# Neighbouring score blocks, earlier normed and turned tiles, and three more fillers in a chunk-attention and Fourier-mix kernel

## The chip, the cores and the metric

The kernel runs on one core of a Trainium2 chip. The metric is the device time of one execution in microseconds. Three runs of the kernel before gave 1109.81 (median), 1108.6 and 1110.18 us. The profiled execution took 1109.99 us, of which 1108.2 us lie between its first and last instruction.

## What is computed

Attention within chunks of 64 tokens, then a mixing block with two Fourier transforms, a normalisation and a two-layer perceptron. All data are float32, with q, k, v of 8 batches x 8 heads x 576 tokens x 64.

```python
scores = scale * matmul(q_c, k_c.T)             # per chunk of 64 tokens
attn   = softmax(scores)
x      = matmul(attn, v_c)                      # then to (B, S, 512)
mixed  = real(fft(fft(x, axis=1), axis=2))
u      = x + mixed
un     = (u - mean(u)) / sqrt(var(u) + 1e-6)
out    = u + relu(un @ w_ch1) @ w_ch2           # 512 -> 2048 -> 512
```

## The kernel before

**Tiles and groups.** Tokens are handled in 36 tiles of 128 (two chunks). A batch has four tiles of its own ("lo" and "hi", two each, since the Fourier transform folds a token with its mirror image), and every two batches share a "rest" tile. Even batches therefore have five tiles in this order and odd ones four. The perceptron works on groups of four tiles: one group for each batch, and a ninth for the four rest tiles.

**Two streams in one program.** The order of every engine's instructions is written out by hand. The loop at L1189 runs the perceptron of group g step by step (`mlp`), and after each step it advances a generator, `side(b)`, that does the attention of batch b (`attention`), three empty steps, and its Fourier part (`fourier`). So the batch g+1 is prepared while group g is in the perceptron. Each engine works its list off in order; semaphores between the engines are set by the framework.

**The perceptron's forms.** Group 0 uses plain products. From group 1 on the down product (`down_halves`, L1042) and from group 2 on the up product (`up_halves`, L997) use seven products of half size instead of eight, numbered o = 0 to 6. Each is done for r = 0 and 1, and k = 2o + r counts these in the down half. A step of the down half is eight float32 matmuls on TensorE, which are 16 passes. The results are summed from PSUM by VectorE and ScalarE, on lines L1018 to L1035 and L1065 to L1082. The operands for the down half are made ahead by `operands` (L916 to L920). Converted weights are written to DRAM by `keep1` and `keep2` during groups 0 and 1, through buffers that share the places `wb` and `yall` with those operands, and fetched again by `fetch`.

**Attention of a tile** (from batch 2 on). `att_T` transposes q and k on VectorE (L348) and loads the next tile's q and k. `att_S` (L380) makes the scores, 32 small passes in a 64x64 mode. `softmax` (L393, L395) takes maximum and difference on VectorE, `exponential` is on ScalarE. `att_P` transposes the weights on TensorE (L329). `att_V` (L428) weights the values, 32 small passes again, into two PSUM buffers of the pool `ps_t`, and VectorE divides (L441 to L445). In the loop of `attention`, the scores of tile n+1 stand right behind the weighting of tile n, except for a batch's first tile, whose scores open the batch's generator.

**From one group to the next.** While group g is in its down half, the tiles of group g+1 are finished: `fourier` adds the mixed part and takes means (L712, L632, L633, with the reciprocal deviation at L637), `normed` (L824) makes `un`, `turned` (L329, then L835 or L837) transposes it through a `ps_t` buffer into `unT`, and `combined` (L845 to L848) makes three sums of it for the seven products. `normed` of tile j is asked for after step k = 4 + 2j, `turned` after step k = 5 + 2j.

**The start.** Batch 0 is done by `attention_early` and `fourier_early`. Where TensorE has nothing to do there, `keep_warm` puts in fillers: matmuls on zeros whose result is not used (L1142).

Of the kernel before, what the change touches and what calls it, by code (L numbers as in the profile page):

```python
# [16 lines left out]
def kernel(  # L17
# [39 lines left out]
    NT = 2 * 2 * NM + 1  # L57
# [315 lines left out]
    def att_S(n):  # L373
        a, b = qT.pop(n), kT.pop(n)
        sc = ps_a.tile([128, 2, 512], FP32, tag="att", name="sc")
        for j in range(NJ):
            for e in range(2):
                for c in range(2):
                    r0, t0 = e * D, c * CH
                    nc.tensor.matmul(  # L380
                        out=sc[t0:t0 + CH, e, j * CH:(j + 1) * CH],
                        lhsT=a[r0:r0 + D, 2 * j + c, 0:CH],
                        rhs=b[r0:r0 + D, 2 * j + c, 0:CH],
                        start=True,
                        stop=True,
                    )
        scs[n] = sc
# [139 lines left out]
    def attention_early():  # L527

        lo, hi = first[0], first[1] - 1

        def ready(n):
            if n == at[LO, 0, 1]:
                shift_early(0)
            if n == at[HI, 0, 1]:
                fold(0, 1)
            if n == at[HI, 0, 0]:
                fold(0, 0)
            if n + 3 > hi:
                load_v(n + 3)

        att_T(lo)
        att_S(lo)
        for n in range(lo, hi + 1):
            if n < hi:
                att_T(n + 1)
            softmax(n)
            if n > lo:
                att_V(n - 1)
                ready(n - 1)
            if n < hi:  # L550
                att_S(n + 1)
            if n in (lo, hi):
                keep_warm(1)
            att_P(n)
        shift_early(1)
        fold(0, NM)
        keep_warm(1)
        att_V(hi)
        ready(hi)
        keep_warm(3)  # L560
        turn_tables()
        round_next()
        round_next(put_off)

    def attention(b):

        lo, hi = first[b], first[b + 1] - 1

        def ready(n):

            if n == at[LO, b, NM - 1]:
                shift(b)
            for i in range(NM):
                if n == at[HI, b, i]:
                    fold(b, i)
            if n == at[HI, b, 0]:
                fold(b, NM)
            return kind(n) == HI

        if b > 1:  # L580


            att_S(lo)
            softmax(lo)
            yield
            for n in range(lo, hi + 1):
                exponential(n)
                if n + 1 < NT:
                    att_T(n + 1, "q")
                yield  # L590
                att_P(n)
                if n + 1 < NT:
                    att_T(n + 1, "k")
                yield
                att_V(n)
                if n < hi:
                    att_S(n + 1)
                    softmax(n + 1)
                if n + 3 < NT:
                    load_v(n + 3)  # L600
                yield ready(n)
            return
        att_T(lo)
        yield
        for n in range(lo, hi + 1):
            att_S(n)
            softmax(n)
            yield
            if n + 1 < NT:
                att_T(n + 1)  # L610
            yield
            if n > lo:
                att_V(n - 1)
                if n + 2 < NT:
                    load_v(n + 2)
                yield ready(n - 1)
            att_P(n)
            yield
        att_V(hi)
        if hi + 3 < NT:  # L620
            load_v(hi + 3)
        yield ready(hi)
# [204 lines left out]
    def turned(g, s):  # L827
        if s >= len(groups[g]):
            return
        if s == 0:  # L830
            unTs[g] = one_p.tile([128, KD, G * 128], FP32, tag="unT", name="unT")
        unT, un = unTs[g], uns.pop((g, s))
        pt = turn(lambda j: un[:, j * 128:(j + 1) * 128])
        if s % 2 and g > 1:
            nc.vector.tensor_copy(unT[:, :, s * 128:(s + 1) * 128], pt)  # L835
        else:
            nc.scalar.copy(unT[:, :, s * 128:(s + 1) * 128], pt)  # L837
# [204 lines left out]
    def down_halves(g, h1):  # L1042
        pas, pbs = {}, {}
        for o in range(NO):
            w = slab2[((g - first_of[2]) * NO + o) % NS2]
            for r in range(2):
                cl, ch = slice(r * 128, (r + 1) * 128), slice(256 + r * 128, 256 + (r + 1) * 128)
                low, high = groups[g][r], groups[g][2 + r]
                olow, ohigh = os_[:, 2 * r], os_[:, 2 * r + 1]
                a, b = tmp[:, r, 0], tmp[:, r, 1]  # L1050
                if o == 0:
                    pas[r] = ps_f.tile([128, 2, 256], FP32, tag="ff", name="pa")
                if o == 2:
                    pbs[r] = ps_f.tile([128, 2, 256], FP32, tag="ff", name="pb")
                dst = (pas, pas, pbs, pbs, pas, pbs, pbs)[o][r][:, (0, 1, 0, 1, 0, 0, 1)[o]]
                lhs = (
                    h1[:, 0:HF, cl], ys[:, :, cl], xs[:, :, cl], h1[:, 0:HF, ch],
                    h1[:, HF:KF, cl], ys[:, :, cl], h1[:, HF:KF, ch],
                )[o]
                for m in range(HF):  # L1060
                    nc.tensor.matmul(  # L1061
                        out=dst, lhsT=lhs[:, m], rhs=w[:, m],
                        start=(o in (0, 2) and m == 0), stop=(m == HF - 1), skip_group_check=True,
                    )
                if o == 0:  # L1065
                    nc.scalar.copy(a, dst)
                elif o == 1:
                    nc.vector.tensor_tensor(out=b, in0=dst, in1=a, op=ALU.add)
                elif o == 2:
                    nc.vector.tensor_tensor(out=a, in0=dst, in1=b, op=ALU.add)  # L1070
                elif o == 3:
                    nc.vector.tensor_tensor(out=ohigh[:, HM:DM], in0=dst, in1=ohigh[:, HM:DM], op=ALU.add)
                    nc.gpsimd.tensor_tensor(out=olow[:, HM:DM], in0=b, in1=natural(low)[:, HM:DM], op=ALU.add)
                    nc.gpsimd.tensor_tensor(out=ohigh[:, 0:HM], in0=b, in1=natural(high)[:, 0:HM], op=ALU.add)
                elif o == 4:
                    nc.vector.tensor_tensor(out=olow[:, 0:HM], in0=dst, in1=natural(low)[:, 0:HM], op=ALU.add)
                elif o == 5:
                    nc.vector.tensor_tensor(out=olow[:, HM:DM], in0=dst, in1=olow[:, HM:DM], op=ALU.add)
                    store(low, olow)
                else:  # L1080
                    nc.vector.tensor_tensor(out=ohigh[:, 0:HM], in0=dst, in1=ohigh[:, 0:HM], op=ALU.add)  # L1081
                    store(high, ohigh)  # L1082
                k = 2 * o + r
                if g + 1 < NG:
                    for j in range(G):
                        if k == 4 + 2 * j:
                            normed(g + 1, j)
                        if k == 5 + 2 * j:
                            turned(g + 1, j)
                            if j >= 2:  # L1090
                                combined(g + 1, j - 2)
                if r == 1:
                    if o == 1:
                        for j in range(0, HF, 2):
                            two = ys[:, j:j + 2]
                            nc.gpsimd.tensor_tensor(
                                out=two, in0=h1[:, HF + j:HF + j + 2, lo], in1=two, op=ALU.subtract
                            )
                    if o == 2:
                        for i in range(2):  # L1100
                            nc.gpsimd.tensor_tensor(
                                out=os_[:, 2 * i + 1, HM:DM], in0=tmp[:, i, 0],
                                in1=natural(groups[g][2 + i])[:, HM:DM], op=ALU.add,
                            )
                    fetch(2)
                yield
# [7 lines left out]
    with tc.manual_schedule():  # L1114
# [24 lines left out]
        def keep_warm(times):  # L1139

            for _ in range(times):
                nc.tensor.matmul(out=idle[:, 0:NQ], lhsT=warm[:, 0:128], rhs=warm[:, 0:NQ], start=True, stop=True)  # L1142
# [130 lines left out]
```

## Time and profile before

| engine | busy, us | share of the span |
|---|---|---|
| TensorE (PE) | 1079.4 | 97% |
| TensorE weight loads (PEld) | 849.1 | 77% |
| VectorE (DVE) | 582.1 | 53% |
| ScalarE (ACT) | 297.5 | 27% |
| GpSimd (POOL) | 277.4 | 25% |

| stretch, us | what runs | PE busy | DVE busy | DMA share |
|---|---|---|---|---|
| 54 to 140 | group 0, weights rounded | 83.36 of 86 | 80.31 | 0.67 |
| 140 to 250 | groups 0 and 1, converted weights stored | 107.93 of 110 | 59.16 | 0.67 |
| 250 to 880 | groups 1 to 6 | 619.17 of 630 | 338.92 | 0.59 |
| 880 to 1108 | groups 7 and 8 | 223.37 of 228 | 73.16 | 0.42 |

An idle engine costs nothing as long as TensorE doesn't wait for it. The granted TensorE clock is full nearly everywhere (0.998 on average). In a timeline row the columns are: start in us, length in us, engine, line, operation, output<-input, shapes, how many instructions were merged, and in brackets the idle time before the first of them with the instruction that ended it. A float32 matmul stands as two passes. "SPq" is the queue that issues most transfers.

### The profile page before, as it was taken

What the parts mean: (1) busy time and instruction counts of PE and PEld (TensorE: products, weight loads), DVE (VectorE), ACT (ScalarE), POOL (GpSimd) and SP (SyncE); (2) the same over time, 40 slices, a digit from 0 to 9 for tenths busy, and PEclk for the clock granted to TensorE, in tenths of its full rate; (3) what the DMA queues carried; (4) which work ended last, traced back from release to release, by engine and by line L of the source; (5) the groups of instructions that cost most, each with busy time, mean ns of one, the idle gap of its engine ahead of it and who ended that gap; (6) DMA issues with size and microseconds to landing.
All of it is one profiled execution on the core that took longest, in us unless ns stands there. A gap on an engine that the chain in (4) does not pass through costs nothing. (4 is left out here: it accounts for less than half of the span.)

```text
span 1108.2 us, 18749 instructions
## 1 busy us (share of the span) xinstructions
PE 1079.4 (97%) x7010; PEld 849.1 (77%) x7010; DVE 582.1 (53%) x1260; ACT 297.5 (27%) x725; POOL 277.4 (25%) x403
## 2 busy tenths in 40 slices
PE   8899999999999999999999999999999999999998
PEld 6644454447887888888888888788888888888887
DVE  4798987325566365663556455625554434323521
ACT  4588453212112311322022212221133102201210
POOL 4200102354405140244024220424042401120130
PEclk9999999999999999999999999999999999999999
DMA  7767656679566546683559357753653355446232
GB/s 169 227 178 193 154 169 229 177 245 287 182 188 191 162 141 199 197 249 108 168 170 251 115 167 211 202 178 132 202 168 111 114 183 178 134 152 200 85 114 76
DMA packets 147970, 192.73 MB, mean 174 GB/s; under 512 B 66126, under 2 KB 104014, under 8 KB 140712
## 3 DMA queue, kind: packets, MB, share of 16 engines
q1 hardware_dynamic: 145620, 190.20, 56.8%
q8 instruction: 56, 0.92, 0.3%
q0 software_dynamic: 512, 0.68, 0.3%
q10 hardware_dynamic: 1748, 0.66, 0.2%
q14 instruction: 34, 0.28, 0.1%
HBM read 167.22 MB, written 24.12 MB: 173 GB/s over the span
## 5 line engine op out<-in xcount | busy, mean ns | idle before, releaser
L920 POOL TENSOR_TENSOR h<-h 128x256 f32<-128x256 f32 x64 | 56.0, 880 | 269.0 <-PE pb L1014 153.1
L1061 PE MATMUL pa<-wb,h 128*128 128x256 f32 x512 | 114.4, 380 | 0.0
L1061 PE MATMUL pb<-wb,h 128*128 128x256 f32 x512 | 114.2, 380 | 0.0
L1014 PE MATMUL pb<-unT,wa 128*128 128x256 f32 x448 | 107.0, 382 | 3.7 <-DVE wa L1023 3.4
L1014 PE MATMUL pb<-wa 128*128 128x256 f32 x448 | 107.2, 382 | 2.6 <-DVE h L1031 2.6
L1061 PEld LDWEIGHTS pa<-wb,h 128*128 128x128 f32 x512 | 96.4, 190 | 13.4 <-issue 0.5
L1014 PE MATMUL pa<-unT,wa 128*128 128x256 f32 x448 | 106.6, 381 | 0.0
L1061 PEld LDWEIGHTS pb<-wb,h 128*128 128x128 f32 x512 | 96.1, 190 | 12.6
L1014 PEld LDWEIGHTS pb<-unT,wa 128*128 128x128 f32 x448 | 84.1, 190 | 19.0 <-DVE wa L1023 8.0
L1014 PEld LDWEIGHTS pb<-wa 128*128 128x128 f32 x448 | 83.8, 190 | 15.4 <-DVE h L1031 3.8
L1014 PEld LDWEIGHTS pa<-unT,wa 128*128 128x128 f32 x448 | 83.9, 190 | 11.1
L930 PE MATMUL up<-unT,wa 128*128 128x512 f32 x128 | 58.0, 600 | 2.0 <-ACT h L938 1.2
L968 PE MATMUL dn<-wb,h 128*128 128x512 f32 x128 | 57.4, 597 | 1.3 <-ACT h L938 1.3
L1061 PE MATMUL pa<-wb,yall 128*128 128x256 f32 x256 | 57.9, 381 | 0.0
L1061 PE MATMUL pb<-wb,yall 128*128 128x256 f32 x256 | 57.1, 381 | 0.0
L947 PE MATMUL up<-unT,wa 128*128 128x512 f32 x128 | 56.8, 596 | 0.0
L1029 ACT ACTIVATE h<-pa 128x256 f32<-128x256 f32 x56 | 21.5, 383 | 131.3 <-PE pa L1014 131.3
L1061 PE MATMUL pb<-wb 128*128 128x256 f32 x256 | 56.6, 379 | 0.0
L1021 DVE TENSOR_TENSOR wa<-pa,wa 128x256 f32<-128x256 f32 x56 | 23.8, 424 | 61.3 <-PE pa L1014 59.6
L1014 PE MATMUL pa<-wa 128*128 128x256 f32 x224 | 53.2, 380 | 0.7 <-ACT wa L1019 0.7
L1061 PEld LDWEIGHTS pb<-wb,yall 128*128 128x128 f32 x256 | 48.1, 190 | 6.5
L1061 PEld LDWEIGHTS pb<-wb 128*128 128x128 f32 x256 | 48.2, 190 | 6.2
(242 smaller groups left out, 1655.7 us busy)
## 6 DMA issues: line engine op xcount, KB each, us to landing
wb<-s SPq DMA_DIRECT2D x56, 1024.0 KB
wa<-s SPq DMA_DIRECT2D x196, 256.0 KB
xall<-in_moe_w_ch_dram SPq DMA_DIRECT2D x22, 512.0 KB
q<-in_q_dram SPq DMA_DIRECT2D x96, 112.0 KB
k<-in_k_dram SPq DMA_DIRECT2D x96, 112.0 KB
v<-in_v_dram SPq DMA_DIRECT2D x124, 64.0 KB
yall<-in_moe_w_ch_dram SPq DMA_DIRECT2D x10, 512.0 KB
s<-wb SPq DMA_DIRECT2D x20, 256.0 KB
```

Of the source, the lines that this page charges most:

```text
L920: nc.gpsimd.tensor_tensor(out=h1[:, m, hi], in0=h1[:, m, lo], in1=h1[:, m, hi], op=ALU.subtract)
L930: nc.tensor.matmul(out=up, lhsT=w1[:, kk, m * 128:(m + 1) * 128], rhs=unT[:, kk], start=(kk == 0), stop=(kk == KD - 1),)
L947: nc.tensor.matmul(out=up, lhsT=w1[:, kk, m * 128:(m + 1) * 128], rhs=unT[:, kk], start=(kk == 0), stop=(kk == KD - 1),)
L968: nc.tensor.matmul(out=dn, lhsT=h1[:, m, s * 128:(s + 1) * 128], rhs=w2[:, m, :], start=(m == 0), stop=(m == KF - 1),)
L1014: nc.tensor.matmul(out=dst, lhsT=w[:, kk, r], rhs=rhs[o][:, kk], start=(o in (0, 2) and kk == 0), stop=(kk == 1), skip_group_check=True,)
L1021: nc.vector.tensor_tensor(out=b, in0=dst, in1=a, op=ALU.add)
L1029: nc.scalar.activation(out=h1[:, m, lo], in_=dst, func=ACTF.Relu)
L1061: nc.tensor.matmul(out=dst, lhsT=lhs[:, m], rhs=w[:, m], start=(o in (0, 2) and m == 0), stop=(m == HF - 1), skip_group_check=True,)
```

## The change

Four edits in one.

- Three more fillers behind the last weighting of `attention_early`, to keep TensorE at work while the tables are turned.
- In `attention`, the scores and softmax of the next batch's first tile are put right behind the last weighting of the batch, so that two blocks in the 64x64 mode stand together. Only batch 2 still opens with its own scores, since batch 1 has another loop.
- In `down_halves`, `normed` of tile j is asked for one step earlier, after k = 3 + 2j, to have it ready when its transposes come up.
- In `down_halves`, `turned` of tile j is asked for in the middle of step k = 5 + 2j, between its fourth and fifth matmul, so that its PSUM buffer is free again sooner. `combined` stays after the step.

The order of the instructions on ScalarE, GpSimd and the SP queue is the same in both programs.

```diff
@@ attention_early
         ready(hi)
-        keep_warm(3)
+        keep_warm(6)
         turn_tables()
@@ attention
         if b > 1:
-            att_S(lo)
-            softmax(lo)
+            if b == 2:
+                att_S(lo)
+                softmax(lo)
             yield
...
                 att_V(n)
-                if n < hi:
+                if n + 1 < NT:
                     att_S(n + 1)
                     softmax(n + 1)
@@ down_halves
+                k = 2 * o + r
                 for m in range(HF):
+                    if m == HF // 2 and g + 1 < NG and k in range(5, 5 + 2 * G, 2):
+                        turned(g + 1, (k - 5) // 2)
                     nc.tensor.matmul(
...
-                k = 2 * o + r
                 if g + 1 < NG:
                     for j in range(G):
-                        if k == 4 + 2 * j:
+                        if k == 3 + 2 * j:
                             normed(g + 1, j)
-                        if k == 5 + 2 * j:
-                            turned(g + 1, j)
-                            if j >= 2:
-                                combined(g + 1, j - 2)
+                        if k == 5 + 2 * j and j >= 2:
+                            combined(g + 1, j - 2)
```

## Prediction

> **What bounds the kernel now.** First the busy table, to see which engine the span is made of.
>
> ```profile
> PE 1079.4 (97%) x7010; PEld 849.1 (77%) x7010; DVE 582.1 (53%) x1260; ACT 297.5 (27%) x725; POOL 277.4 (25%) x403
> ```
>
> TensorE is busy for 97% of 1108.2 us, so a change is worth what it takes from, or adds to, TensorE's own stream. Next, what TensorE waited for (total us, times, longest):
>
> ```profile
> PE pb L1014 <- DVE wa L1023: 3.4, 6, 0.9
> ...
> PE xp L428 <- ACT unT L837: 2.5, 6, 0.4
> PE z L740 <- POOL pm_rest L522: 2.4, 1, 2.4
> PE pt L329 <- DVE un L824: 2.1, 7, 0.4
> PE sc L380 <- DVE rd L441: 1.7, 1, 1.7
> ```
>
> The third row is the target of the fillers, the second and fourth of the earlier normed and turned tiles. These waits are counted from modelled ends; from start to start they are a little longer, and I use those. Third, the windows around the third row's wait (us; busy PE, PEld, DVE, ACT, POOL; clock; DMA share; GB/s):
>
> ```profile
> 29.70:33.07 3.37, 1.00 (x5) 0.87 (x5) 3.27 (x8) 2.12 (x6) 2.87 (x6) 1.00 0.78 208
> 33.07:36.49 3.42, 3.42 (x15) 1.91 (x14) 0.48 (x2) 1.97 (x3) 2.07 (x8) 0.50 0.97 376
> ```
>
> A stretch with 30% of TensorE work is followed by 3.4 us at half clock. Fourth, the timeline where batch 2 hands over to batch 3, for TensorE and VectorE:
>
> ```profile
> 230.56 0.69 PE L380 MATMUL sc<-kT,qT 64*64 64x64 f32 x32 [1.65 <-DVE rd L441]
> ...
> 242.12 0.70 PE L428 MATMUL xp<-v,pT 64*64 64x65 f32 x32
> ```
>
> ```profile
> 229.43 1.08 DVE L348 STREAM_TRANSPOSE kT<-k 128x512 f32<-128x512 f32 x1 [6.43 <-DMA k<-in_k_dram]
> ...
> 247.01 0.53 DVE L918 TENSOR_TENSOR wb<-h 128x256 f32<-128x256 f32 x1 [14.03 <-DMA s<-wb]
> 247.57 0.43 DVE L919 TENSOR_TENSOR yall<-wb,h 128x256 f32<-128x256 f32 x1
> 247.91 1.10 DVE L348 STREAM_TRANSPOSE qT<-q 128x512 f32<-128x512 f32 x1
> ...
> 251.79 1.10 DVE L348 STREAM_TRANSPOSE kT<-k 128x512 f32<-128x512 f32 x1 [2.06 <-DMA k<-in_k_dram]
> ```
>
> Weighting 242.12 is the last of batch 2. The transposed keys of the next tile, batch 3's first, come at 251.79 + 1.10 = 252.9, because VectorE stands 14.03 us behind a store of converted weights and then 2.06 us behind the load of k. Before the change the scores that read them are at 286.42, so nobody cares.
>
> [...] scores at 230.56 wait for the keys transposed from 229.43 to 230.51, and the up matmuls behind them wait too. [...] a block of scores alone adds 0.72 us to the stream (0.20 from the last transpose start instead of 0.11, then 0.62), a block of weightings alone 0.72, but the two as neighbours 1.19.
>
> **The change, part by part.**
>
> *Three more fillers (L560).* A filler is two passes, starts 0.243 us apart, so three are 1.46 us. They stand in the stretch from 29.7 to 32.07, where TensorE waited 2.37 us; the tables that end that wait come from ScalarE, which is not touched. Cost nothing. The window then holds 2.5 of 3.4 us of work instead of 1.0. If this counts as busy, the half-clock window goes. It cost this: the first z group with its mid rows, 32.07 to 35.55, took 3.48 against 2.28 in the next (37.56 to 39.84), and the six filler passes after it 2.01 against 1.46: 1.2 + 0.55, less 0.2 for VectorE, whose weight rounding ends at 39.35 before it can copy z. Bounds 0 and -1.8; I take **-1.6**, since scores, means and the first up matmuls follow in one chain.
>
> *Normed tiles sooner.* un(0) was issued behind the block of means of the second pair, which waits 1.45 us for GpSimd, so it came at 522.58 and its transposes at 523.26, where the 32 passes from 515.87 end at 522.78. Now it stands before that block, after L1068 at 515.68; its rstd is ready at 516.33. It is then done at 516.9, over 4 us before need. It delays the block by 0.1 us, which the eviction L1070 has room for. Six such waits from start to start, 0.38 to 0.49: **-2.7**. The other un tiles also move up and have more room than before.
>
> *Turned tiles inside a step.* Same transposes, same number. At 302.37 the weighting waits for its second PSUM buffer until ScalarE has copied unT (0.58 us from 302.48): the 32 passes take 1.16 instead of 0.52. With eight passes (1.7 us) between transposes and weighting the copy is over. Five places: **-3.1**. The VectorE copies of odd tiles come before an eviction that has not its data yet; the combines follow the copies as before. Nothing.
>
> *Neighbours.* Five pairs (ends of batches 2 to 6): 0.72 + 0.72 - 1.19 = 0.25 each: **-1.3**. What moves with the scores is their softmax on VectorE, 0.68 + 0.69 us. In the down half it was hidden under 32 passes of 6.9 us. In the up half the matmuls of product 3 wait for L1023 behind it. With scores at 336.87 these matmuls come 3.74 us after the weighting began; without them, at 352.48, 2.50 after. Take off 0.47 for the scores: 0.8 for each of batches 3 and 5. Batches 4 and 6 end after product 5; scores there (465.03) led to a wait of 0.53 for ScalarE's L1019. Sum 2 x 0.8 + 2 x 0.53: **+2.7**. In the plain up loop of batch 2 ScalarE evicts: nothing.
>
> *The wait that this adds.* TensorE now meets the first scores of batch 3 right behind weighting 242.12, at 242.7, and its keys are there at 252.95. Behind the scores in TensorE's queue stand all remaining up matmuls (13.57 us of them) and the down half. VectorE's wait is for stores and loads that the SP queue issues in an order that doesn't change (k at 246.29), and nothing TensorE does after 242 helps: **+10.3**. If the SP queue doesn't follow the 1.6 us gained at the start, 11.9. For batches 3 to 6 the keys are ready 0.9 to 2.2 us before (350.84 for 353.0, 478.4 for 479.9, 589.8 for 590.7, 716.3 for 717.9): nothing, though 0.9 us is thin.
>
> *The clock after it.* [...] 3.4 to 6.8 us at half speed, 1.7 to 3.4 us lost. I take **+2.3**.
>
> Sum: -1.6 - 2.7 - 3.1 - 1.3 + 2.7 + 10.3 + 2.3 = **+6.6**; 1109.8 + 6.6 = 1116.4 us.
>
> **Rivals.** (a) *The keys are in time*: VectorE's 14 us wait shrinks with the shifted start and the scores don't block. Then the last two terms go: 1109.8 - 6.0 = 1103.8, faster. Against it: the scores at 230.56 already had to wait, and the load of k is issued 3.6 us after the weighting. Chance 0.06. (b) *Part of the wait only*: the stores land earlier, TensorE waits 5 us, loses 1.7 to the clock: 1109.8 - 6.0 + 6.7 = 1110.5, no change. From 240 to 260 us the DMA engines are 0.97 busy, so nothing there lands early; 0.07. (c) *Worse*: the SP queue stays where it is (+1.6), the clock loss is 3.4 and one of the thin margins fails: about 1119.5. Chance 0.19. (d) *The forecast*, with its terms off by one or two us in sum: 0.68.
>
> **How the numbers follow.** The time is that of (d), 1116.4. Its unknowns are the clock (1.7 to 3.4), the fillers (0 to -1.8), the stall (9.5 to 11.9) and the half-stage waits (1.5 to 3.5): 1113 to 1119. Down to 1112.6 and up to 1119.5 leaves out (a), most of (b) and a little of (c). Slower by over 0.2% (above 1112.0): (d), (c) and some of (b), 0.89. Within it 0.05, faster 0.06.
>
> **What would show it.** A wait of the scores for kT near 242 of some 10 us, as the longest row of TensorE's waits; a window at half clock after it; none from 33 to 36. Rows for un and for unT before the weighting all but gone; the L1023 wait grown by about 1.6 us, an L1019 wait by 1. If the keys' transpose near 252 ends before the scores' turn, or the waiting VectorE instruction is another one that the change frees, the forecast falls.

## The result, and the profile after

| | before | after |
|---|---|---|
| time, us (median of 6 runs each) | 1109.8 (1107.41 to 1112.54) | 1116.84 (1114.78 to 1117.2) |
| span of the profiled execution, us | 1108.2 | 1115.1 |
| mean granted TensorE clock | 0.998 | 0.995 |

The ratio is 1.006, with a 95% interval from 1.0044 to 1.0076: the change makes the kernel slower by some 7 us. The forecast was 1116.4.

The busy table of the kernel after, which answers to the one shown of before (busy us, share of the span, instructions):

```profile
PE 1078.4 (97%) x7016; PEld 847.5 (76%) x7016; DVE 579.3 (52%) x1260; ACT 296.3 (27%) x725; POOL 280.3 (25%) x403
```

TensorE has six passes more (the three fillers) and is busy for 1.0 us less. The span is 6.9 us longer. So the loss lies in waits, and the next view to read is the list of what TensorE waited for (total us, times, longest). Line numbers behind the edited lines are up to four higher than in the kernel before.

```profile
PE sc L380 <- DVE kT L348: 10.5, 1, 10.5
PE pb L1015 <- DVE wa L1024: 4.6, 8, 0.7
...
PE pa L1015 <- ACT wa L1020: 1.5, 4, 0.4
...
PE z L741 <- POOL pm_rest L522: 1.3, 1, 1.3
...
PE xp L428 <- ACT unT L838: 0.4, 1, 0.4
PE pt L329 <- DVE un L825: 0.4, 1, 0.4
```

The two rows at the bottom were 2.5 and 2.1 us before: the step edits did what they are for. The row at the top is new, a single wait of 10.5 us. The second and third rows grew (from 3.4 us in 6 waits; from 0.7 us in 2). Now the place of the new wait, in the timelines of TensorE and of VectorE, kernel after:

```profile
241.31 0.70 PE L428 MATMUL xp<-v,pT 64*64 64x65 f32 x32
252.54 1.13 PE L380 MATMUL sc<-kT,qT 64*64 64x64 f32 x32 [10.53 <-DVE kT L348]
253.60 15.91 PE L948 MATMUL up<-unT,wa 128*128 128x512 f32 x32
```

```profile
245.28 0.53 DVE L919 TENSOR_TENSOR wb<-h 128x256 f32<-128x256 f32 x1 [13.12 <-DMA s<-wb]
...
251.32 1.08 DVE L348 STREAM_TRANSPOSE kT<-k 128x512 f32<-128x512 f32 x1 [3.24 <-DMA k<-in_k_dram]
```

Weighting 241.31 is batch 2's last. Batch 3's first scores now stand behind it, and their keys are transposed only by 252.40, because VectorE was held by the store at L919 and then by the load of k, as in the kernel before. The up matmuls at 253.60 need neither (in the kernel before they ran on from 242.75), but they come next in TensorE's queue.

What follows the wait is seen in windows of the kernel after (us; busy PE, PEld, DVE, ACT, POOL with counts; granted clock; DMA share; GB/s):

```profile
29.70:33.07 3.37, 2.04 (x9) 1.35 (x8) 3.17 (x8) 2.12 (x6) 3.08 (x6) 1.00 0.68 208
33.07:36.49 3.42, 3.42 (x21) 2.36 (x21) 0.86 (x4) 1.97 (x3) 0.17 (x1) 1.00 0.92 323
...
247.25:252.54 5.29, 0.00 (x1) 0.03 (x1) 2.02 (x5) 0.00 (x0) 1.16 (x2) 0.50 0.95 288
252.54:257.49 4.95, 4.95 (x37) 2.77 (x38) 4.11 (x11) 0.00 (x0) 4.16 (x7) 0.50 1.01 421
257.49:265.00 7.51, 7.51 (x18) 3.25 (x18) 1.70 (x4) 1.20 (x2) 4.11 (x6) 1.00 0.77 174
```

The half-clock stretch at 33 us, which the profile before had, is gone. A new one runs from 247.25 to 257.49. Its first half falls into the wait and costs nothing; its second covers 4.95 us of work. In it the up matmuls from 254.61 on start 0.85 us apart, and at full clock, from 257.76 on, 0.43 us apart, so by estimate about half of the 4.95 us, 2.5 us, are lost.

### The profile page after: what moved, and what is told of

It reads as the page before. It is cut to its first block, busy times and chain, and to the rows that moved or that the text cites. A ratio compares the mean times of both kernels' runs of the same rounds, so it can differ in the third digit from the quotient of the medians.

```text
span 1115.1 us, 18767 instructions
## 1 busy us (share of the span) xinstructions
PE 1078.4 (97%) x7016; PEld 847.5 (76%) x7016; DVE 579.3 (52%) x1260; ACT 296.3 (27%) x725; POOL 280.3 (25%) x403
## 4 chain that ended last, share of the span: by engine, by line
PE 74%; DMA 8%; DVE 7%; issue 3%; SPq 3%; ACT 2%; POOL 2%; DVEq 0%; POOLq 0%; ACTq 0%
PE pb L1065 19%; PE pa L1065 15%; PE pb L1015 14%; PE pa L1015 11%; PE dn L969 3%; PE pt L329 2%; PE up L931 2%; PE more_z L648 2%; PE mix L696 2%; PE z L648 2%; DMA wa<-s 2%; PE up L948 1%; DMA q<-in_q_dram 1%; DMA xall<-in_moe_w_ch_dram 1%; PE xp L428 1%
## 5 line engine op out<-in xcount | busy, mean ns | idle before, releaser
L713 POOL TENSOR_TENSOR xall<-y,xall 128x513 f32<-128x513 f32 x14 | 21.3, 1519 | 128.1 <-DVE y L707 128.1
L1065 PEld LDWEIGHTS pa<-wb,yall 128*128 128x128 f32 x256 | 47.7, 190 | 6.4
```

The costliest lines, as they stand in the source:

```text
L713: eng.tensor_tensor(out=x[:, 0:w], in0=y[:, 0:w], in1=x[:, 0:w], op=ALU.add)
L1065: nc.tensor.matmul(out=dst, lhsT=lhs[:, m], rhs=w[:, m], start=(o in (0, 2) and m == 0), stop=(m == HF - 1), skip_group_check=True,)
```

## The experiments

The theory was that of the prediction: the step edits save about 6 us, the neighbours edit loses about 14, of which 12 to 13 come from one stall (the wait for the keys and the clock after it). The rivals on trial were that the loss belongs to the step edits or to the softmax in the half stages, that the clock costs nothing of its own, and that the late keys are only a matter of the SP queue or only of VectorE. "The rest" below is the time from the start of the first up matmul of group 0 to the end of the last matmul, read from the profiled executions: it leaves out the start, whose length varies by 2 us between executions (the first up matmul stands at 51.67 in the earliest and 54.01 in the latest profile). It is one execution of each kernel: before (1049.4) and fillers_only (1048.0) run the same instructions in it and differ by 1.4 us, so a difference of that size is not clear of noise.

### One part at a time

**fillers_only**: before, with one edit.

```diff
-        keep_warm(3)
+        keep_warm(6)
```

> Before plus the three fillers alone. Theory: the half-clock window from 33 to 36.5 us goes and the first up matmul (54.01 us) starts up to 1.6 us sooner, 1108.2 us. In the profile of the changed kernel that window is gone, but the first up matmul still starts at 53.88, since the tables came later in that execution; if that is the rule, 1109.7. Rival, fillers stand in the way: the first z product starts later than 32.1 because of them, over 1110.

Measured: 1108.5 us against 1108.65, ratio 1.000 [0.999, 1.001]. No gain, although the profile shows the clock full throughout (1.000 in the mean). The timeline of fillers_only around 40 us shows what set the pace:

```profile
38.15 0.49 DVE L305 TENSOR_SCALAR wa<-yall 128x512 uint32<-128x512 uint32 x1 [3.72 <-DMA yall<-in_moe_w_ch_dram]
...
40.54 0.69 DVE L319 TENSOR_TENSOR wa<-wa,power 128x512 f32<-128x512 f32 x1
...
41.15 0.42 DVE L750 COPY zf<-z 128x256 f32<-128x256 f32 x1
...
41.62 1.62 PE L770 MATMUL early_xp<-start,zf 128*128 128x256 f32 x6 [0.66 <-DVE zf L750]
```

TensorE waits for a copy that stands on VectorE behind the rounding of a block of weights, and that block landed at 38.15; in the profile before it landed at 36.57. The first up matmul follows at 53.93, before at 54.01. Among the profiles, two of the five kernels with three fillers have the half-clock window near 33 us (before and neighbours_only), and none of the eight with six. Over the executions, the mean clock is 0.998 or lower in 15 of 42 of the kernel before and in 1 of 14 of fillers_only. One 3.41 us window at half clock lowers the mean of 1108 us by 0.0015; the clock also falls behind the last matmul (at 1114.24 of 1115.1 us in after), but with that counted, seven profiles that are at full clock from 29.70 to 39.80 us have means of 0.999 or 1.000. So the fillers do remove the window, but most executions of before don't have it, and in the profile of fillers_only, where the weights land late, the time gained is spent waiting for VectorE.

**steps_only**: before, with the two edits in `down_halves`, three fillers.

```diff
+                    if m == HF // 2 and g + 1 < NG and k in range(5, 5 + 2 * G, 2):
+                        turned(g + 1, (k - 5) // 2)
...
-                        if k == 4 + 2 * j:
+                        if k == 3 + 2 * j:
                             normed(g + 1, j)
```

> Before plus the earlier normed and turned tiles alone. Theory: six waits for un (2.7 us) and five for unT ahead of the weighting (3.1 us) go, 1104.0 us. Rival, transposes in the middle of a product cost something (its passes are cut in two, an accumulation is interrupted): with 28 such cuts at 0.2 us or more the gain is gone, 1109.6 or above.

Measured: 1102.3, ratio 0.9934 [0.9919, 0.9949]. The rest is 1041.6 us: 6.3 less than in fillers_only and 7.7 less than in before. In TensorE's waits of steps_only, the rows of the two targets (2.5 and 2.1 us before):

```profile
PE xp L428 <- ACT unT L837: 0.4, 1, 0.4
PE pt L329 <- DVE un L824: 0.4, 1, 0.4
```

One short wait of each is left; six and five are gone.

**neighbours_only**: before, with the edit in `attention`.

```diff
-            att_S(lo)
-            softmax(lo)
+            if b == 2:
+                att_S(lo)
+                softmax(lo)
...
-                if n < hi:
+                if n + 1 < NT:
```

> Before plus the neighbouring blocks alone. Theory: -1.3 for five pairs, +2.7 for softmax in the half stage, +10.3 for the scores that wait for the keys of batch 3, +2.3 for the clock: 1123.8 us. Rival, the pairs are harmless and the loss of the changed kernel comes from the cut steps: about 1108.5.

Measured: 1123.65, ratio 1.0126 [1.0108, 1.0144]; the rest is 14.3 us longer than before's. TensorE's waits in neighbours_only:

```profile
PE sc L380 <- DVE kT L348: 10.2, 1, 10.2
PE pb L1015 <- DVE wa L1024: 5.5, 8, 0.9
...
PE pa L1015 <- ACT wa L1020: 1.5, 4, 0.4
```

The stall and both grown half-stage rows belong to this edit alone, with a half-clock stretch of 10.24 us from 246.81.

**all_but_neighbours**: after, without the edit in `attention`.

> The changed kernel with the neighbouring blocks taken back. Theory: fillers and steps remain, -5.8 and 0 to -1.6: 1102.4 to 1104.0 us, no TensorE wait over 2 us after 54 us. Rival (cut steps cost): 1109 or more.

Measured: 1100.96, ratio 0.9925 [0.991, 0.9939]. This beats both kernels; steps_only, within the intervals, is no different. So the whole loss is in the neighbours edit, and the step edits are not part of it.

### The step edits taken apart

**normed_only**: before with `k == 3 + 2 * j` for `normed`, `turned` left after the step.

> Before with normed one step earlier and turned where it was. Theory: the six waits for un go, those for unT stay: 2.7 us under before (0.9976). Rival, un takes VectorE's time from evictions that TensorE waits for: no change.

Measured: 1106.61, ratio 0.9975 [0.9964, 0.9985], which is 2.8 us. The waits of normed_only keep the row that this half doesn't touch:

```profile
PE xp L428 <- ACT unT L837: 2.5, 6, 0.4
```

**turned_only**: before with `turned` in the middle of the step, `normed` left after k = 4 + 2j.

> Before with turned in the middle of a step and normed where it was. Theory: the five waits for unT go (-3.3), but un of tile 0 comes as late as before and its transposes are asked for four matmuls (1.72 us) sooner, so six waits of 0.45 become 2.2 each (+10.3): 7 us over before (1.006). Rival, un waits are set by the place of its transposes only, not by VectorE's block of means: 3 us under before.

Measured: 1118.7, ratio 1.0087 [1.0072, 1.0101]: slower. The waits of turned_only say why:

```profile
PE pt L329 <- DVE un L824: 12.4, 7, 2.1
```

The transposes moved up by half a step, but what they read did not; six waits of about 2 us take the place of six of 0.4. The two halves of this edit don't add up (2.8 us gained, 9.4 lost; together 6.3 gained): either can be judged only with the other. The time is also above what was expected (9.4 us over before, where 7 was). The windows of turned_only show what adds to it (columns as above):

```profile
760.00:764.74 4.74, 2.70 (x15) 2.12 (x14) 2.08 (x6) 0.84 (x3) 2.77 (x3) 1.00 0.00 0
764.74:768.16 3.42, 3.42 (x39) 2.39 (x37) 0.42 (x1) 0.24 (x1) 0.34 (x1) 0.50 0.00 0
...
884.21:887.62 3.41, 3.41 (x11) 2.70 (x10) 0.00 (x0) 0.58 (x1) 0.00 (x0) 0.50 0.00 0
```

Each half-clock window follows one wait, of 2.04 us at 761.69 and of 1.94 us at 881.79, in a stream that is dense otherwise. By estimate, half of each window of 3.41 us, 1.7 us, is lost, 3.4 together.

### The stall taken apart

**batch3_own_scores**: after, with batch 3 opening with its own scores again; the other four pairs stay.

```diff
-            if b == 2:
+            if b in (2, 3):
...
-                if n + 1 < NT:
+                if n + 1 < NT and n + 1 != first[3]:
```

> The changed kernel, except that batch 3, like batch 2, opens with its own scores. Theory: the wait of 10.5 us and the half-clock stretch behind it go and the other four pairs stay: steps -6.3, fillers 0, four pairs -1.0 + 2.7, so 4.6 us under before (ratio 0.996). Rival, the 15 us of the neighbouring blocks are spread over their five places at 3 us each: 5.6 us over before (1.005).

Measured: 1103.19, ratio 0.9944 [0.9931, 0.9957]. The rest is 1043.2 us: 13.1 below after's 1056.4, so that is the price of the one pair. It is also 1.6 above steps_only's and 3.1 above all_but_neighbours' (1040.2): the other four pairs lose, by an amount that is little more than the noise of the rest. TensorE's waits in batch3_own_scores:

```profile
PE pb L1015 <- DVE wa L1024: 4.9, 8, 0.9
...
PE pa L1015 <- ACT wa L1020: 1.5, 4, 0.4
```

Both rows stay as grown as in after, with no row for the keys. Four of the waits in them come behind the four pairs, at 353.35 and 589.14 for VectorE and at 481.12 and 717.24 for ScalarE. From start to start they add 0.83, 0.75, 0.53 and 0.54 us to the 1.89 and 1.72 us that the same eight passes take without a wait.

**warm_wait**: after, with 19 fillers on TensorE ahead of batch 3's first scores, where it has to wait anyway.

```diff
+                if n + 1 == first[3]:
+                    hold = ps_f.tile([128, 512], FP32, tag="ff", name="hold")
+                    for _ in range(19):
+                        nc.tensor.matmul(
+                            out=hold[:, 0:NQ], lhsT=warm[:, 0:128], rhs=warm[:, 0:NQ], start=True, stop=True
+                        )
                 if n + 1 < NT:
```

> The changed kernel with 19 fillers (38 passes at 0.243, 9.2 us) between the last weighting of batch 2 and the first scores of batch 3, so that TensorE waits as long but at work. Theory: the keys come when they came, the clock stays whole, and the time falls by the clock's share alone, 2.3 us (2.0 to 2.9): 4.5 us over before (1.004). Rival, the clock costs nothing here since all waits on the keys anyway: as the changed kernel, 7 us over before (1.006).

Measured: 1113.02, ratio 1.0039 [1.0025, 1.0054]. TensorE's timeline in warm_wait:

```profile
239.88 9.52 PE L600 MATMUL hold<-warm 128*128 128x289 f32 x38
250.39 0.70 PE L380 MATMUL sc<-kT,qT 64*64 64x64 f32 x32 [0.99 <-DVE kT L348]
```

The scores come no earlier after the weighting, the clock stays full (1.000 in the mean, 0.995 in after), and they take 0.70 us where after's took 1.13. The rest falls by 2.4 us: this is the clock's share of the loss, apart from the wait's.

**k_from_act_queue**: after, with the load of k for batch 3's first tile issued from ScalarE's queue instead of SP's.

```diff
-... (k, ks, "k", nc.scalar if n == 0 else nc.sync) ...
+... (k, ks, "k", nc.scalar if n in (0, first[3]) else nc.sync) ...
```

> The changed kernel with k of batch 3's first tile issued by ScalarE's queue, so that it doesn't stand behind the stores of converted weights. Theory: the wait has two parts in a row, VectorE behind the store (to 245.3 us) and then the load of k; with the load early the keys come right after the queries and one pair of operands, about 249.5 instead of 252.4: the wait falls from 10.5 to 7.5 us, 3 us under the changed kernel. Rival, the load of k alone sets it: the wait all but goes, 12 us under the changed kernel.

Measured: 1114.2, ratio 1.0041 [1.0026, 1.0056]. VectorE's timeline in k_from_act_queue:

```profile
245.80 0.50 DVE L919 TENSOR_TENSOR wb<-h 128x256 f32<-128x256 f32 x1 [14.70 <-DMA s<-wb]
...
248.40 1.08 DVE L348 STREAM_TRANSPOSE kT<-k 128x512 f32<-128x512 f32 x1
```

The keys no longer wait for their load, but still stand behind L919, whose wait for the store grew by 1.6 us. TensorE waits 8.7 us instead of 10.5. The rest, 1056.4, is no shorter than after's, though: in this execution the two largest rows of waits in the up half are together 1.7 us longer (5.8 and 3.1 against 4.6 and 2.6).

**operands_late**: after, with group 1's `operands` (L919 and its kind) made after the up loop instead of within it, so that VectorE is not held by the store; the load of k stays on SP.

```diff
-            if g >= first_of[2] and m > HF:
-                operands(h1, m - HF - 1)
             yield h1
         if g >= first_of[2]:
-            operands(h1, HF - 1)
+            for m in range(HF):
+                operands(h1, m)
```

> The changed kernel with group 1's operands (L919 to L921) all made after its up loop, so that VectorE doesn't stand behind the store of converted weights. Theory: the keys still wait for the load of k, which lands at about 251.3, so TensorE's wait stays at 10 to 10.5 us; the operands then come late for the down half and may add 0 to 5 us. Rival, the 13 us wait of VectorE for the store is what holds the keys: the wait falls to 3 us or less.

Measured: 1115.5, ratio 1.0051 [1.0036, 1.0066]. VectorE's timeline in operands_late:

```profile
242.35 1.10 DVE L348 STREAM_TRANSPOSE qT<-q 128x512 f32<-128x512 f32 x1 [11.50 <-DMA q<-in_q_dram]
250.33 1.08 DVE L348 STREAM_TRANSPOSE kT<-k 128x512 f32<-128x512 f32 x1 [6.87 <-DMA k<-in_k_dram]
```

With the store out of the way, VectorE waits for the loads instead, and the keys come 1 us earlier than in after. TensorE waits 11.0 us (the row names rd L441, which ends together with the keys, at 251.4), from a weighting that itself is 1.5 us earlier. The rest is the same as after's, so the later operands cost nothing that shows.

**keys_early**: after, with both of these edits at once; q of this tile also from ScalarE's queue, and its one-column copy on VectorE instead of GpSimd.

> Both of these, and q of that tile from ScalarE's queue too, and its one-column copy on VectorE instead of GpSimd. Theory: nothing is left in front of the keys, the scores of batch 3 follow the weighting at 241.9 without a wait and the clock stays whole: 12.5 us under the changed kernel, less what the late operands cost (0 to 5), so 7.5 to 12.5 us under it. Rival, the place itself costs (another wait steps in): less than 4 us under it.

Measured: 1104.85, ratio 0.996 [0.9943, 0.9978]. TensorE's timeline in keys_early:

```profile
242.51 0.70 PE L428 MATMUL xp<-v,pT 64*64 64x65 f32 x32
243.02 0.65 PE L380 MATMUL sc<-kT,qT 64*64 64x64 f32 x32
```

The pair now runs with no wait and the clock stays full (1.000 in the mean). So two chains held the keys: their own load behind SP's queue, to 251.4 us even without the store (operands_late), and the store ahead of them on VectorE, to 249.5 us even with the load early (k_from_act_queue). Freeing one uncovers the other, and neither alone is enough. Whether the queue of q and the moved copy of one column were needed too was not tried alone. Even so, this version is not faster than batch3_own_scores, where the pair doesn't exist: its scores at 230.94, of batch 2, wait 2.6 us for VectorE (a row of 0.6 there), and its rest is 2.0 us longer.

## Why the prediction was right

Its forecast of 1116.4 is 0.4 us from the measured median. The mechanism held, one long wait for the keys and the clock after it against the gain of the step edits. That the number came so close is in part luck, since errors of the terms were made up for by the spread between executions. Step by step, with the rest as the measure:

| term | predicted, us | measured, us | from |
|---|---|---|---|
| fillers | -1.6 | 0 (-1.1 to +1.1) | fillers_only's ratio |
| un ready sooner, turned sooner | -2.7 - 3.1 = -5.8 | -6.3 (-7.7) | steps_only against fillers_only (against before) |
| four pairs and their softmax | -1.0 + 2.7 = +1.7 | +1.6 (+3.1) | batch3_own_scores against steps_only (against all_but_neighbours) |
| fifth pair: its saving, stall and clock | -0.25 + 10.3 + 2.3 = +12.3 | +13.1 | after against batch3_own_scores |
| of it, the clock | +2.3 | +2.4 | after against warm_wait |

- **Fillers: the mis-sized term.** The working took the half-clock window of one profile as present in every execution and as lying on the chain to the first up matmul; of its bounds, 0 and -1.8, the runs gave the upper one. They showed the window in about a third of the executions, and in one profile a chain that ends in VectorE's rounding of weights that landed late. In each of the three sets of runs of before, the executions at 0.998 or lower take on average 1.4 to 2.3 us longer than the others, about the size of the term. A third of that would be 0.5 to 0.8 us, which the interval of fillers_only allows, so rarity alone can be the reason; how much is hidden besides isn't settled. The mechanism, more work in the window and no half clock after it, was right. The stretch of 3.37 us ahead of the drop had 1.00 us of work in the kernel before and 2.54 in fillers_only, where no drop followed. How much work is enough was not shown: the same stretch held 1.09 us in normed_only without a drop, and in turned_only half clock came after 1.37 and 1.47 us of work in 3.41 (last section).
- **Normed and turned.** Right in mechanism and in size: -2.8 for the first alone. That the prediction summed them as separate terms was harmless, but turned_only shows that the second term holds only with the first in place.
- **Pairs and half stages.** Right in size and sign. The four waits come where the working put them and add 2.6 us (0.8 twice and 0.53 twice were worked out). The saving of a pair was not measured apart from them, and the sum, +1.6 or +3.1 by the run that it is held against, is near the noise.
- **The stall.** Predicted at 10.3, it is 10.5 us by the list of waits. The instructions named as its cause, the store ahead on VectorE and the load of k, are the ones that keys_early had to free; operands_late and k_from_act_queue show that freeing either one alone leaves a wait of 11.0 or 8.7 us. Behind the waiting scores the up matmuls, whose like ran on from 242.75 in the kernel before, started at 253.60, 1.06 us after the scores.
- **The clock.** 2.4 us, shown apart from the wait by warm_wait. The half-clock stretch is 10.24 us long, three times the 3.41 us of the one in the kernel before. The working allowed 3.4 to 6.8 us of it after the wait, once or twice that length, which was the author's estimate; it was 4.95 us, and the rest fell into the wait.
- **Rivals.** "The keys are in time" gave 1103.8, which is about what the chip does once they are (keys_early at 0.996 of before: 4.4 us less; the prediction had 6.0, of which 1.6 were the fillers). "Part of the wait only" and "worse" did not come: the wait was 10.5 us and not 5, the clock cost 2.4, and no other pair waits for its keys in the list of after.

The forecast's errors in the fillers (1.6 too low), the fifth pair (0.8 too low), the steps (0.5 too high) and the four pairs (0.1 too high) add up to 1.8 us too low; it missed by 0.4. The difference is the 1.4 us by which the rests of before and fillers_only differ, although both run the same instructions in it.

## What to carry to other kernels

Before moving a small block forward on the busiest engine, whose next instructions here stood behind it for 10.5 us, look up in the old trace when each of its operands is ready, and what stands ahead of their producer; where the old place gave slack, the wait without it is the first cost of the new one, here about ten times the 1.3 us that the pairs could save. When an operand is late, follow every chain to it before freeing one: here there were two, and freeing either one left at least 8.7 of the 10.5 us. A long stall on TensorE is to be charged with the half clock that the trace shows after it, here 2.4 us beside a wait of 10.5, and a gain read off one clock window of one profile should first be checked for how many executions have it.

## What the hardware showed that was not expected

- A wait of about 2 us was enough for half clock in some places and not in others, and its length alone doesn't tell which. Four waits with a drop behind them, and two without:

| run | wait, us | its end | TensorE work in the 3.41 us up to the drop, us | half clock from |
|---|---|---|---|---|
| before | 2.37 | 32.07 | 1.04 | 33.07 |
| neighbours_only | 2.08 | 31.60 | 1.34 | 31.77 |
| turned_only | 2.04 | 763.74 | 1.37 | 764.74 |
| turned_only | 1.94 | 883.73 | 1.47 | 884.21 |
| normed_only | 2.28 | 32.28 | - | none |
| turned_only | 2.26 | 32.57 | - | none |

- So of the six waits of about 2 us for un in turned_only, two were followed by 3.41 us at half clock. Two such stretches lower the mean of its 1116.6 us by 0.003, three would by 0.0046, and the mean was 0.997. The wait near 30 us led to half clock in two of the five profiles with three fillers. Why some of these waits did and others didn't was not shown. The work is counted by modelled ends of matmuls.
- The half-clock stretches ahead of the last matmul were 3.41 us long in before and turned_only, and 10.24 us in after and neighbours_only.
- In the long wait of after the clock fell 5.2 us after the wait had begun (242.01 to 247.25) and came back 4.95 us after the work had (252.54 to 257.49), so only half of the 10.24 us cost anything.
- With 19 fillers ahead of the wait the clock was full behind it: the scores took 0.70 us in warm_wait and 1.13 in after.
